# Attention and two expert layers on one core: second halves of x on GpSimd one a unit, a group split later, its four pieces in another order

## The chip, the cores and the metric

The kernel runs on one core of a Trainium2 chip. The metric is device time in microseconds (us), the median over the runs of one kernel. The core has TensorE (PE, with its weight loads as PEld), VectorE (DVE), ScalarE (ACT), GpSimd (POOL) and the queue that issues the DMAs (SP). Each engine works through its own instructions strictly in the order in which the program emits them, so an instruction that waits holds up all that stands behind it on that engine.

## The reference

```python
attn_out = _attn_ref(q, k, v, w1, b1, w2)             # 2 batches, 8 heads, 576 rows, 64 columns
x = attn_out.transpose(0, 2, 1, 3).reshape(1152, 512)
# first layer: w_in 512x2048 and w_out 2048x512
h = x @ w_in
P = a[0] + a[1]*h + a[2]*h**2 + a[3]*h**3
Q = 1.0 + abs(b[0])*abs(h) + abs(b[1])*h**2
x = (P / (Q + 1e-6)) @ w_out
# second layer: 4 experts, w1[e] 512x1024 and w2[e] 1024x512
p = domain_probs / (domain_probs.sum(-1, keepdims=True) + 1e-9)
for e in range(4):
    out += p[:, e:e+1] * (np.maximum(x @ w1[e], 0) @ w2[e])
```

## The kernel before

Every product is made of three: each factor is held as a first part (a copy rounded by ScalarE) and a second part (the factor less its first part, one subtraction on VectorE or GpSimd), and PE adds first*first, first*second and second*first. The change is about who makes second parts, and when.

**The first layer** (loop at L855 and on) has 24 units, each a chunk of 384 tokens (chunks 0 to 2) by 256 of the 2048 inner columns. In unit i PE makes the 24 products `hp` (L56) of x and w_in, and the 24 `yp` of unit i-2. ACT and DVE turn `hp` into g (`chain`, L760 to L777); its last DVE instruction (L777) is the last that reads `hp`, and `hp` has two buffers, so the products of unit i+1 wait for L777 of unit i-1. One weight is split in each unit (`convert`: ACT L369, then the second part in L375). POOL makes the second part of g (L757). The last three f2 of the units go through chunk 2, then 1, then 0. When a chunk's last unit ends (`gather`, L816), DVE adds up its four column blocks d (L826), and `result` (L837) makes the two parts of the new x: ACT L839, then DVE L840. Chunk 2's four results are put into the list `later` and run at the end of that same unit (L874); chunk 1's four and two of chunk 0 are put into `results`, and are taken out one after each of the first three pieces of work of the experts 1 and 2 (L970). The chunk 2 results must be there before the first expert's products.

**The second layer, chunk 2** (loop at L965): for each expert u, `expert_first(u, f2)` makes 24 products `hp` for 256 inner columns, with ACT L847 (`h_hi`) and DVE L848 (`h_lo`) behind them, the last readers of `hp`. Expert u+1's f2 = 0 is made ahead. Then `expert_second(u, t)` makes 24 products `op` for each of three token tiles t, and DVE L896 adds them into `acc`. For the last expert t = 0 and 1 are interleaved: 18 products of each, then 6 of each, then the 24 of t = 2. Two buffers of `hp` again: the products of f2 wait for `h_lo` of f2-2.

**Splitting weights ahead.** Between these, `turns(n)` emits the next n steps of the list `order`; how many stands in `PACE`, three numbers for the places behind `expert_first` 1 to 3 and three for those behind `expert_second` 0 to 2. A weight (`Weight`) is one step: ACT L369, then DVE L375, and then the load of the next but one into the buffer (`stage`, two of them) that this frees. A `Group` holds four blocks of w1[e], for one square below, and is split in five steps (`Group.work`, L400): step 0, ACT L406 and L407 (waits for four DMAs, issued at L398); step 1, three subtractions on DVE or POOL (L410); step 2, four subtractions on POOL, L412 to L415, that turn the four blocks into their sums; step 3, ACT L417 of all four sums; step 4, their second parts, L420: one DVE instruction, or four pieces on POOL in the order 0, 1, 2, 3.

For expert 2 PACE is (2, 1, 1, 3, 3, 3), for expert 3 (2, 2, 2, 2, 1, 2). Around the change this gives, in emission order (W3 are weights of expert 3, G0, G1, G2 the first three groups):

- second layer, expert 2, t = 0; first sums of x (`sums_of_x`: DVE, POOL, DVE, DVE); split of W3 in 3, out 0, out 1
- expert 2, t = 1; split of W3 out 2; G0 steps 0 and 1
- expert 2, t = 2; G0 steps 2, 3 and 4
- expert 3, f2 = 1 (`hp`, `h_hi`, `h_lo`); split of W3 out 3; G1 step 0
- f2 = 2; G1 steps 1 and 2
- f2 = 3; G1 steps 3 and 4
- t = 0 and 1, 18 products each; t = 0, 6 products and its L896; copies of the sums (ACT L954, six); G2 steps 0 and 1
- t = 1, 6 products and its L896; second parts of the sums (DVE L957, six); G2 step 2
- t = 2, 24 products and its L896; G2 steps 3 and 4
- the squares

**The second layer, chunks 0 and 1** (loop at L1064) goes by one level of Strassen's scheme: for each of four experts four squares g, each of seven products m of six matmuls (`Square`, L1001; `sa`, `sb`, `sc`, L1025). They run in the order 1, 6, 7, 2, 5, and 3, 4 of a square after 1, 6 of the next. Product 2 is added onto `sa` and so waits until ACT L1047 has copied product 1; product 5 is added onto `sb` after DVE L1049. Products 6, 7, 5 and 4 use the pieces 3, 1, 0 and 2 of step 4 (`RIGHT`). The fourth group of each expert is split on POOL just ahead of its square.

Of the kernel before, what the change touches and what calls it, by code (L numbers as in the profile page):

```python
# [15 lines left out]
ALU = mybir.AluOpType  # L16
# [31 lines left out]
def attention_then_two_ffn(ctx: ExitStack, tc: tile.TileContext, q, k, v, w1, b1, w2, w_in, w_out, ca, cb, probs, e_w1, e_w2, c_l, c_l8, c_p, c_x, out):  # L48
    nc = tc.nc
    act, dve, pool, pe, sp = nc.scalar, nc.vector, nc.gpsimd, nc.tensor, nc.sync  # L50

    def f32(ap):
        return ap.bitcast(F32)
# [117 lines left out]
    later = []  # L171

    def catch_up(calls):
        now, calls[:] = calls[:], []
        for f in now:
            f()
# [200 lines left out]
    class Group:  # L377
# [22 lines left out]
        def work(self, step, eng):  # L400

            b, s, raw = self.b, self.s, self.raw
            n = 4 if eng is dve else 1
            b11, b12, b21, b22 = (raw[:, i] for i in range(4))
            if step == 0:
                act.activation(b[:, 0, 0], b11, AF.Copy)  # L406
                act.activation(b[:, 2:4, 0], raw[:, 2:4], AF.Copy)  # L407
            if step == 1:
                for i in (0, 2, 3):
                    eng.tensor_tensor(b[:, i, 1], raw[:, i], f32(b[:, i, 0]), ALU.subtract)  # L410
            if step == 2:
                pool.tensor_tensor(b11, b12, b11, ALU.subtract)  # L412
                pool.tensor_tensor(b12, b22, b12, ALU.subtract)  # L413
                pool.tensor_tensor(b22, b22, b11, ALU.subtract)  # L414
                pool.tensor_tensor(b21, b21, b22, ALU.subtract)  # L415
            if step == 3:
                act.activation(s[:, :, 0], raw, AF.Copy)  # L417
            if step == 4:
                for i in range(0, 4, n):
                    eng.tensor_tensor(s[:, i:i + n, 1], raw[:, i:i + n], f32(s[:, i:i + n, 0]), ALU.subtract)  # L420

    W1 = [(Weight(w_in, f2, False), Weight(w_out, f2, True)) for f2 in range(DFF // 256)]
# [30 lines left out]
    def convert(steps=5):  # L453

        for _ in range(steps):
            if state["step"] == 0 and not can_convert():
                return
            i = state["done"]
            if isinstance(order[i], Group):
                if state["step"] == 0:  # L460
                    order[i].place()
                order[i].work(state["step"], side[0])
                state["step"] = (state["step"] + 1) % 5
                if state["step"] == 0:
                    under_way.pop(i)
                    state["done"] += 1
                    load_ahead()
            elif state["step"] < 4:
                under_way[i].narrow(state["step"])
                state["step"] += 1  # L470
            else:
                order[i].place()
                under_way.pop(i).split()
                state["step"] = 0
                state["done"] += 1
                load_ahead()
# [6 lines left out]
    x_t = {}  # L483
# [24 lines left out]
    class Pair:  # L508
# [69 lines left out]
        def parts(self, x):  # L578

            o = self.o  # L580
            yield x[:, 0:512].rearrange("p (k a i) -> p a k i", a=4, i=32), o[:, :, 32:160].rearrange("p a (k i) -> p a k i", i=32)
            for e in range(2):
                r, c = slice(64 * e, 64 * e + 64), 160 * (1 - e)
                yield x[r, 512:S].rearrange("p (a i) -> p a i", i=32), o[r, 2 * e:2 * e + 2, c:c + 32]
# [114 lines left out]
    units = [(n, u) for n in range(NN) for u in range(9)]  # L699
    units[:11] = [(0, u) for u in (0, 1, 2, 3, 4, 5, 8)] + [(1, 0), (1, 1), (0, 6), (0, 7)]  # L700
    for i in range(-2, len(units)):
        if i + 2 < len(units):
            n, u = units[i + 2]
# [5 lines left out]
        if 0 <= i + 1 < len(units):  # L709
            n, u = units[i + 1]  # L710
            pair[n].exp(u)
        if i >= 0:
            n, u = units[i]
# [9 lines left out]
    def first(w, c):  # L723

        wt = ready(w)
        w.left -= 1
        hp = ps.tile([P, 2, 512], F32, tag="s", name="hp")
        for fi in range(2):
            i = 0
            for cc in range(4):  # L730
                for wpart, xpart in ((0, 0), (0, 1), (1, 0)):
                    mm(hp[:, fi, :CHN], wt[:, cc, wpart, 128 * fi:128 * fi + 128], x_t[cc][:, c, xpart], i == 0, i == 11)
                    i += 1
        return hp[:, :, :CHN]
# [4 lines left out]
    units = [(c, f2) for grp in range(NGRP) for c in (range(3), range(2, -1, -1))[grp % 2] for f2 in GROUPS[grp]]  # L739
    CHUNKS = range(3) if NGRP % 2 else range(2, -1, -1)  # L740
# [5 lines left out]
    results = []  # L746
# [13 lines left out]
    def chain(i, h, tile):  # L760

        qd, u, r = tile("qd"), tile("u"), tile("r")
        act.activation(qd, h, AF.Abs, scale=abs_b[:, 1:2])
        act.activation(u, h, AF.Identity, scale=nca[:, 3:4], bias=nca[:, 2:3])
        yield
        dve.scalar_tensor_tensor(out=qd, in0=qd, scalar=abs_b[:, 0:1], in1=h, op0=ALU.add, op1=ALU.mult)
        dve.tensor_tensor(u, h, u, ALU.mult)
        dve.scalar_tensor_tensor(out=u, in0=u, scalar=nca[:, 1:2], in1=h, op0=ALU.add, op1=ALU.mult)
        act.activation(qd, qd, AF.Abs)
        act.activation(r, qd, AF.Ln, bias=one)  # L770

        act.activation(h, r, AF.Exp, scale=-1.0)
        yield

        dve.scalar_tensor_tensor(out=qd, in0=qd, scalar=1.0 + 1e-6, in1=h, op0=ALU.add, op1=ALU.mult)
        dve.scalar_tensor_tensor(out=h, in0=u, scalar=nca[:, 0:1], in1=h, op0=ALU.add, op1=ALU.mult)
        dve.scalar_tensor_tensor(out=u, in0=qd, scalar=-2.0, in1=h, op0=ALU.add, op1=ALU.mult)  # L777
        g_of[i] = u
        yield
# [20 lines left out]
    def tmp(name, dt=F32):  # L800
        return mp.tile([P, 2, CHN], dt, tag="g", name=name, bufs=13)
# [14 lines left out]
    def gather(i):  # L816
        c, f2 = units[i]
        if i not in ends:
            return
        yp = y_of.pop(c)  # L820
        for d in range(4):
            ya = yacc[:, d, CHN * c:CHN * c + CHN]
            if i == first_end[c]:
                act.activation(ya, yp[d][:, :CHN], AF.Copy, scale=1 / WUP)  # L824
            elif i == last_end[c]:
                dve.scalar_tensor_tensor(out=ya, in0=yp[d][:, :CHN], scalar=1 / WUP, in1=ya, op0=ALU.mult, op1=ALU.add)  # L826
                if c != CHUNKS[2] or d > 1:
                    (later if c == CHUNKS[0] else results).append(lambda ya=ya, yt=x_t[d][:, c]: result(ya, yt))
            else:
                if d % 2 == 0:  # L830
                    new = tmp("y")
                act.activation(new[:, d % 2], yp[d][:, :CHN], AF.Copy, scale=1 / WUP)  # L832
                if d % 2:
                    ya = yacc[:, d - 1:d + 1, CHN * c:CHN * c + CHN]
                    pool.tensor_tensor(ya, ya, new, ALU.add)

    def result(ya, yt):  # L837

        act.activation(yt[:, 0], ya, AF.Copy)  # L839
        dve.tensor_tensor(yt[:, 1], ya, f32(yt[:, 0]), ALU.subtract)  # L840

    h_of = {}

    def expert_first(u, f2):
        h = first(W2[u][f2][0], CHUNKS[0])
        hi, lo = tmp("h_hi", F32R), tmp("h_lo", F32R)
        act.activation(hi, h, AF.Relu)  # L847
        dve.scalar_tensor_tensor(out=lo, in0=h, scalar=0.0, in1=f32(hi), op0=ALU.max, op1=ALU.subtract)  # L848
        h_of[u, f2] = hi, lo
# [3 lines left out]
    for i in range(1, len(units) + LAG):  # L853
        on = i < len(units)
        if on:  # L855
            c, f2 = units[i]
            steps = chain(i, first(W1[f2][0], c), tmp)
            next(steps)
        if i <= len(units):
            parts(i - 1)  # L860
        if on:
            convert(STEPS[i][0])
            next(steps)
            convert(STEPS[i][1])
        if not on:

            expert_first(0, i - len(units))
        if i >= LAG:
            second(i - LAG)
            gather(i - LAG)  # L870
        if on:
            next(steps)
            convert(STEPS[i][2])
            catch_up(later)  # L874

    catch_up(later)

    pr_sb = const.tile([P, NT // P, E], F32, name="pr_sb")
    for j in range(NT // P):
# [47 lines left out]
    def turns(n):  # L927

        for _ in range(n):
            if state["done"] < len(order) and state["step"] == 0 and isinstance(order[state["done"]], Weight) and can_convert():  # L930
                state["step"] = 4
            convert(1)
# [28 lines left out]
    for i, a in enumerate((acc_01[:, 0], acc_01[:, 1], acc_2[:, 0])):  # L961
        acc_of[CHN // P * CHUNKS[0] + i] = a

    PACE = {0: (2, 2, 1, 1, 1, 2), 1: (2, 1, 1, 1, 1, 2), 2: (2, 1, 1, 3, 3, 3), 3: (2, 2, 2, 2, 1, 2)}
    for u in range(E):  # L965
        for f2 in range(1, 4):
            if (u, f2) != (0, 1):
                expert_first(u, f2)
            turns(PACE.get(u, PACE[1])[f2 - 1])
            if 0 < u < E - 1 and results:  # L970
# [3 lines left out]
        for t in range(3):  # L974
# [4 lines left out]
            if (u, t) in ((E - 2, 0), (E - 1, 0), (E - 1, 1)):  # L979
                next(making)  # L980
            turns(PACE.get(u, PACE[1])[3 + t])

# [161 lines left out]
```

## Time and profile before

| | |
|---|---|
| median of 3 runs | 796.0 us (793.53 to 797.44) |
| profiled execution, its time | 792.57 us |
| its span in the trace | 790.8 us (1.77 us lie around it) |
| PE busy | 762.3 us |
| DVE, ACT, POOL busy | 558.0, 429.3, 255.2 us |
| granted TensorE clock, mean | 0.998 |

The span is cut by engine; a group of instructions that follow one another on one engine shows as one row with its count. "Idle before" is the time an engine stood still ahead of a row, and the arrow names what ended it.

### The profile page before, as it was taken

To read this page: it belongs to the slowest core of one execution; us is meant where nothing else is said; L and a number is where in the kernel's file an instruction comes from. 1 tells how busy PE (TensorE), PEld (TensorE's weight loads), DVE (VectorE), ACT (ScalarE), POOL (GpSimd) and SP (SyncE) were. 2 spreads that over 40 slices of the span, in tenths; PEclk is the share of its full clock that TensorE was granted. 3 is DMA by queue.
4 is the path that set the end of the run, shared out by engine and by line. 5 is a ranking of instruction groups with operands and counts; after the bars stand their busy time and mean duration, and the time that the engine had idled before them with its cause. 6 is when DMAs were issued, how large, how long until landed. Compare 5 with 4: busy or idle time off the path is not lost. (4 is left out here: it accounts for less than half of the span.)

```text
span 790.8 us, 15912 instructions
## 1 busy us (share of the span) xinstructions
PE 762.3 (96%) x6470; PEld 659.3 (83%) x6470; DVE 558.0 (71%) x883; ACT 429.3 (54%) x689; POOL 255.2 (32%) x268
## 2 busy tenths in 40 slices
PE   8998999989999999999999999899999999999998
PEld 5445666758899999999998989789889989988987
DVE  7988879996999999999854635647545545644631
ACT  6986657765888889786733524234414323413410
POOL 0000223541453656541100000136436534723710
PEclk9999999999999999999999999999999999999999
DMA  8899586551241231401224533332212202212201
GB/s 148 189 219 211 116 199 160 140 110 46 81 133 54 97 117 59 155 13 50 72 81 133 154 110 110 113 100 94 80 54 81 79 29 81 81 42 77 69 27 54
DMA packets 83945, 79.41 MB, mean 100 GB/s; under 512 B 38016, under 2 KB 62976, under 8 KB 83200
## 3 DMA queue, kind: packets, MB, share of 16 engines
q1 hardware_dynamic: 83440, 78.39, 36.5%
q8 instruction: 51, 0.84, 0.4%
q14 instruction: 22, 0.18, 0.1%
q10 hardware_dynamic: 432, 0.01, 0.0%
HBM read 59.20 MB, written 2.36 MB: 78 GB/s over the span
## 5 line engine op out<-in xcount | busy, mean ns | idle before, releaser
L56 PE MATMUL hp<-x,wi 128*128 128x384 f32 x888 | 161.4, 339 | 6.4 <-DVE h_lo L848 3.6
L56 PEld LDWEIGHTS hp<-x,wi 128*128 128x128 f32 x888 | 155.5, 190 | 9.5 <-DVE h_lo L848 3.9
L56 PE MATMUL op<-w,h 128*128 128x512 f32 (+1 forms) x600 | 133.1, 382 | 0.6 <-DVE acc L896 0.6
L56 PEld LDWEIGHTS op<-w,h 128*128 128x128 f32 x600 | 109.5, 188 | 22.4 <-DVE acc L896 0.8
L56 PE MATMUL yp<-g_hi,w 128*128 128x384 f32 x384 | 102.1, 336 | 0.3 <-ACT y L832 0.3
L896 DVE SCALAR_TENSOR_TENSOR acc<-op,pr_sb,acc 128x512 f32<-128x512 f32 (+1 forms) x28 | 20.4, 730 | 73.9 <-PE op L56 73.9
L56 PEld LDWEIGHTS yp<-g_hi,w 128*128 128x128 f32 x384 | 69.7, 188 | 1.3 <-ACT yacc L824 0.6
L536 ACT ACTIVATE pq<-pq,nm 128x576 f32<-128x576 f32 x72 | 55.4, 772 | 22.5 <-DVE nm L527 22.2
L757 POOL TENSOR_TENSOR g_lo<-u,g_hi 128x768 fp32r<-128x768 f32 x24 | 45.2, 1885 | 62.4 <-ACT g_hi L756 55.9
L56 PE MATMUL yp<-g_lo,w 128*128 128x384 f32 x192 | 64.2, 334 | 0.0
L527 DVE CUSTOM_DVE_ANT_0 pq<-sc,ba 128x576 f32<-128x576 f32 x72 | 51.4, 745 | 16.2 <-PE sc L56 16.1
L56 PE MATMUL sc<-ks,qs 64*128 64x288 f32 (+1 forms) x320 | 56.5, 429 | 6.3 <-DVE nm L527 4.7
L373 POOL TENSOR_TENSOR w<-stage,w 128x256 fp32r<-128x256 f32 x64 | 48.1, 782 | 40.0 <-ACT w L369 40.0
L417 ACT ACTIVATE wi<-stage 128x1024 fp32r<-128x1024 f32 x16 | 17.0, 1061 | 80.3 <-POOL stage L415 80.3
L56 PE MATMUL op<-w,h_hi 128*128 128x512 f32 x192 | 59.2, 389 | 0.0
L369 ACT ACTIVATE w<-stage 128x1024 fp32r<-128x1024 f32 x32 | 33.6, 1054 | 36.8 <-DMA stage<-in_moe_w_dram 36.8
L543 DVE STREAM_TRANSPOSE pt<-pq 128x576 f32<-128x576 f32 x72 | 52.3, 753 | 0.0
L576 PE MATMUL o<-pt,val 32*64 32x128 f32 (+1 forms) x2304 | 48.9, 293 | 2.6 <-issue 1.4
L576 PEld LDWEIGHTS o<-pt,val 32*64 32x64 f32 x2304 | 39.3, 130 | 13.1 <-issue 5.2
L1037 ACT ACTIVATE h<-part_sums 128x384 fp32r<-128x384 f32 x48 | 25.1, 522 | 46.2 <-DVE part_sums L1057 36.9
L232 PE MATMUL bps<-hid,wb 128*32 128x288 f32 x576 | 46.9, 410 | 3.3 <-DVE hid L221 2.4
L56 PEld LDWEIGHTS sc<-ks,qs 64*128 64x128 f32 (+1 forms) x320 | 29.8, 175 | 23.2 <-DVE nm L527 10.2
(141 smaller groups left out, 1441.2 us busy)
## 6 DMA issues: line engine op xcount, KB each, us to landing
stage<-in_moe_w_dram SPq DMA_DIRECT2D x48, 512.0 KB, 3.5
ba<-ev SPq DMA_DIRECT2D x32, 288.0 KB, 5.3
words<-in_moe_w_in_dram SPq DMA_DIRECT2D x8, 1024.0 KB, 5.6
words<-in_moe_w_out_dram SPq DMA_DIRECT2D x8, 1024.0 KB, 4.9
stage<-in_moe_w_dram SPq DMA_DIRECT2D x64, 128.0 KB, 2.4
val<-val SPq DMA_DIRECT2D x21, 288.0 KB, 4.0
val<-in_v_dram SPq DMA_DIRECT2D x11, 288.0 KB, 4.7
out_dram<-acc SPq DMA_DIRECT2D x8, 256.0 KB, 2.0
```

The source lines that it names most:

```text
L56: pe.matmul(o, lhsT=l, rhs=r, start=start, stop=stop)
L232: pe.matmul(sc[32 * par:32 * par + 32, hf, :288], lhsT=wb.rearrange("p r h -> p (r h)"), rhs=tiles[par][:, 288 * hf:288 * hf + 288], start ...
L369: act.activation(t[:, :, 0, :], self.raw, AF.Copy)
L373: pool.tensor_tensor(t[:, x[0], 1, x[1]], self.raw[:, x[0], x[1]], f32(t[:, x[0], 0, x[1]]), ALU.subtract)
L417: act.activation(s[:, :, 0], raw, AF.Copy)
L527: dve.tensor_tensor_reduce(out=self.row(u + e).rearrange("p (a j) -> p a j", a=2), in0=o[:, :, :288], in1=bs.rearrange("p (a j) -> p a j", ...
L536: act.activation(self.row(u), self.row(u), AF.Exp, bias=least.pop((self.n, u)), scale=-1.0, accum_out=self.sm[:, u:u + 1])
L543: dve.transpose(self.pt[:, 5 * e + k], self.row(u))
L576: pe.matmul(self.o[64 * e:64 * e + 64, a, c:c + 32 * m], lhsT=val[self.n % 2][r, NKB * e + b], rhs=self.pt[r, i:i + m, 32 * b:32 * b + 32] ...
L757: pool.tensor_tensor(lo, u, f32(hi), ALU.subtract)
L896: dve.scalar_tensor_tensor(out=a, in0=op, scalar=pr_sb[:, j, e:e + 1], in1=a, op0=ALU.mult, op1=ALU.add)
L1037: act.activation(t[:, 0], v, AF.Relu)
```

## The change

Three things: `result` makes the second part on POOL, and all results go through one list, from which one is taken at the end of each unit from the nineteenth on; PACE of the experts 2 and 3; the order of the four pieces of step 4 on POOL.

```diff
             if step == 4:
-                for i in range(0, 4, n):
+                for i in (0,) if n == 4 else (3, 1, 0, 2):
                     eng.tensor_tensor(s[:, i:i + n, 1], raw[:, i:i + n], f32(s[:, i:i + n, 0]), ALU.subtract)
...
                 if c != CHUNKS[2] or d > 1:
-                    (later if c == CHUNKS[0] else results).append(lambda ya=ya, yt=x_t[d][:, c]: result(ya, yt))
+                    results.append(lambda ya=ya, yt=x_t[d][:, c]: result(ya, yt))
...
         act.activation(yt[:, 0], ya, AF.Copy)
-        dve.tensor_tensor(yt[:, 1], ya, f32(yt[:, 0]), ALU.subtract)
+        pool.tensor_tensor(yt[:, 1], ya, f32(yt[:, 0]), ALU.subtract)
...
             convert(STEPS[i][2])
-            catch_up(later)
-
-    catch_up(later)
+            if results and i < len(units):
+                results.pop(0)()
...
-    PACE = {0: (2, 2, 1, 1, 1, 2), 1: (2, 1, 1, 1, 1, 2), 2: (2, 1, 1, 3, 3, 3), 3: (2, 2, 2, 2, 1, 2)}
+    PACE = {0: (2, 2, 1, 1, 1, 2), 1: (2, 1, 1, 1, 1, 2), 2: (2, 1, 1, 2, 2, 3), 3: (2, 2, 2, 2, 3, 2)}
```

## Rows read from the trace of the kernel before

**Rows 1.** Waits of PE: what it waited for, us in total, times, longest.

```profile
PE hp L56 <- DVE h_lo L848: 3.6, 1, 3.6
PE hp L56 <- DVE u L777: 3.3, 5, 1.4
...
PE sb L1025 <- POOL wi L420: 2.1, 4, 0.5
```

**Rows 2.** Timeline of PE, first layer, units of chunk 1: start, us, what.

```profile
354.37 4.33 PE L56 MATMUL hp<-x,wi 128*128 128x384 f32 x24
362.71 4.33 PE L56 MATMUL hp<-x,wi 128*128 128x384 f32 x24
...
381.09 4.33 PE L56 MATMUL hp<-x,wi 128*128 128x384 f32 x24
```

**Rows 3.** Timeline of DVE in the same units.

```profile
362.23 3.62 DVE L840 TENSOR_TENSOR x<-yacc,x 128x384 fp32r<-128x384 f32 x4
...
371.55 0.95 DVE L777 SCALAR_TENSOR_TENSOR u<-qd,hp 128x768 f32<-128x768 f32 x1
```

**Rows 4.** The ten instructions of L840, their durations in ns (min, median, max).

```profile
L840 DVE TENSOR_TENSOR x<-yacc,x x10: 547/551/2214, 362.2 to 484.0; 128x384 fp32r<-128x384 f32 x10
```

**Rows 5.** Timeline of POOL beside them.

```profile
362.55 1.94 POOL L757 TENSOR_TENSOR g_lo<-u,g_hi 128x768 fp32r<-128x768 f32 x1 [7.12 <-ACT g_hi L756]
```

**Rows 6.** POOL's groups by shape: count, busy us, mean ns of one.

```profile
L598 POOL TENSOR_TENSOR x<-x,x 128x384 fp32r<-128x384 f32 x7 | 7.1, 1019 | 0.6
```

**Rows 7.** Timeline of PE, experts 2 and 3 to the first square.

```profile
501.08 8.49 PE L56 MATMUL hp<-x,wi 128*128 128x384 f32 x48
513.17 6.00 PE L56 MATMUL hp<-x,wi 128*128 128x384 f32 x24 [3.60 <-DVE h_lo L848]
519.00 0.63 PE L56 MATMUL op<-w,h_hi 128*128 128x512 f32 x2
...
535.37 1.21 PE L1025 MATMUL sa<-x,wi 128*128 128x384 f32 x6
```

**Rows 8.** Windows: us, busy PE, PEld, DVE, ACT, POOL, granted clock, DMA share, GB/s.

```profile
514.00:519.00 5.00, 5.00 (x21) 5.00 (x21) 1.64 (x4) 1.75 (x3) 0.00 (x0) 0.68 0.64 182
```

**Rows 9.** Timeline of ACT from expert 3 to the first square.

```profile
506.71 0.63 ACT L407 ACTIVATE wi<-stage 128x512 fp32r<-128x512 f32 x1 [1.31 <-DMA stage<-in_moe_w_dram]
...
510.89 0.79 ACT L847 ACTIVATE h_hi<-hp 128x768 fp32r<-128x768 f32 x1
...
534.23 1.06 ACT L417 ACTIVATE wi<-stage 128x1024 fp32r<-128x1024 f32 x1 [6.83 <-POOL stage L415]
...
536.61 0.49 ACT L1047 ACTIVATE part_sums<-sa 128x384 f32<-128x384 f32 x1 [1.32 <-PE sa L1025]
```

**Rows 10.** Timeline of DVE in the same stretch.

```profile
507.37 0.81 DVE L410 TENSOR_TENSOR wi<-stage,wi 128x256 fp32r<-128x256 f32 x2 [1.52 <-ACT wi L407]
...
512.16 0.95 DVE L848 SCALAR_TENSOR_TENSOR h_lo<-hp,h_hi 128x768 fp32r<-128x768 f32 x1
...
518.48 1.66 DVE L410 TENSOR_TENSOR wi<-stage,wi 128x256 fp32r<-128x256 f32 x3
...
528.76 0.75 DVE L896 SCALAR_TENSOR_TENSOR acc<-op,pr_sb,acc 128x512 f32<-128x512 f32 x1 [4.06 <-PE op L56]
529.43 1.63 DVE L410 TENSOR_TENSOR wi<-stage,wi 128x256 fp32r<-128x256 f32 x3
...
531.65 3.83 DVE L957 TENSOR_TENSOR s<-yacc,s 128x768 fp32r<-128x768 f32 x4
...
537.00 1.21 DVE L420 TENSOR_TENSOR wi<-stage,wi 128x1024 fp32r<-128x1024 f32 x1
```

**Rows 11.** Timeline of POOL in the same stretch: the last sum of G1, then of G2.

```profile
521.63 0.73 POOL L415 TENSOR_TENSOR stage<-stage 128x256 f32<-128x256 f32 x1
...
533.26 0.93 POOL L415 TENSOR_TENSOR stage<-stage 128x256 f32<-128x256 f32 x1
```

**Rows 12.** Timeline of PE, product 6 of the fourth square and the product behind it.

```profile
556.17 0.51 PE L1025 MATMUL sb<-s,wi 128*128 128x384 f32 x2
...
558.01 1.21 PE L1025 MATMUL sb<-x,wi 128*128 128x384 f32 x6
```

## The prediction

> **What bounds the kernel now.** PE, busy for 762.3 of the 790.8 us of the span; its three products for one are the work, and the change takes none of them away. So a gain can only come from time in which PE stands still or runs slowly. I read first the waits of PE [rows 1]: the one for `h_lo` (3.6 us, once), the five for L777 (3.3 us, the longest 1.4) and the four for POOL's L420 (2.1 us). Each of the three parts of the change touches one of these. Then I read PE's own timeline at each place, from start to start, because the lost time is more than the wait shows: a restart costs a little, and the clock can fall.
>
> - First layer: a unit takes 362.71 - 354.37 = 8.34 us, yet from 362.71 to 381.09 two units take 18.38, 1.70 too many [rows 2]. DVE explains it: four L840 fill 3.62 us, and L777, for which PE waits, ends only at 372.50 [rows 3].
> - Expert 3: from 501.08 to the first square at 535.37 lie 34.29 us [rows 7]. 48 `hp` last 8.49 and 24 last 4.33 [rows 2, 7], so 24 take 4.16 in a row, and the three sets 12.48. The 72 `op` take 535.37 - 519.00 = 16.37, or 0.227 each. Together 28.85: 5.44 us are lost, 3.60 standing and 6.00 - 4.33 = 1.67 in the 24 products behind the wait [rows 7], over which the granted clock was 0.68, a stretch partly at the lower level of 1.2 GHz and partly at 2.4 [rows 8].
> - Squares: product 6 of the fourth square takes 558.01 - 556.17 = 1.84 us [rows 12] where six matmuls take 1.04 (a quarter of 4.16), so 0.80 is lost, four times 3.2 us.
>
> **Part 1, results on POOL.** It removes ten L840 of 0.55 us from DVE and adds ten instructions of the same shape to POOL, 1.02 us each by L598, which has that shape [rows 6]; ACT's ten copies stay, and no DMA moves. POOL has the room: it stood still for 7.12 us ahead of its L757 [rows 5]. Chunk 2's four now run in four successive units, so in the unit that stalls L777 ends 3.5 us sooner (3.62 less the overlap with its neighbour), at 369.0. PE wants `hp` at 362.71 + 8.34 = 371.05: 2.1 us of room, and the 1.70 is gone. The last chunk 2 result comes in unit 22, more than a unit ahead of the first expert's products: nothing waits for it. What is late next in these units is nothing I can see. Unknown is what POOL's instructions do to DVE's: one of the L840 took 2.21 us instead of 0.55 [rows 4], and it stood beside POOL's L757 at 362.55 to 364.49 [rows 5]. So the bounds are nothing below and 5 x 1.02 = 5.1 us of DVE delay above, 3.0 beyond the room. I take 0, since DVE's only instruction with two inputs in SBUF left in a unit, L375, stands behind L777, while POOL's instruction follows ACT's copy right behind the first part of the same weight, and so should be over by then.
>
> By the Trainium skill (SBUF — State Buffer, section "SBUF: two separate sides") GpSimd and a VectorE instruction with two SBUF inputs lock each other out of a shared port pair for whole instructions. That speaks against this part. The 2.21 us of L840 agrees with it; by it the sum below would lose up to those 3.0 us.
>
> **Part 2, the group later.** With PACE 2 and 2 for 3 and 3, and 3 for 1, the order becomes: t = 0, W3 in 3 and out 0; t = 1, out 1 and out 2; t = 2, G0 steps 0 to 2; f2 = 1; G0 steps 3 and 4; f2 = 2; out 3 and G1 step 0; f2 = 3; G1 steps 1 and 2; t = 0, copies L954, G1 steps 3 and 4; t = 1, L957, G2 steps 0 to 2; t = 2, G2 steps 3 and 4. Work and DMAs are the same; the loads on SP follow the same freed buffers, and only one write of output passes ahead of one of them.
>
> *What goes.* `h_hi` ran at 510.89 because ACT had L417 ahead of it, which waited for POOL's sums [rows 9]; `h_lo` followed at 512.16 [rows 10]. Now ahead of them stand only L407, ending at 507.34, and L410, ending at 508.18. So `h_hi` ends at 507.34 + 0.79 = 508.13 and `h_lo` at 508.18 + 0.95 = 509.13. PE is through with f2 = 2 at 501.08 + 2 x 4.16 = 509.40: in time by 0.27 us, so 5.44 are saved and the squares could begin at 529.93.
>
> *What is late next.* G2. Its L410 stood ahead of the six L957 and now stands behind them. Six products after 36 put L896 of t = 0 at 513.56 + 42 x 0.227 = 523.1. Then DVE does, back to back: L896 0.67 (528.76 to 529.43 [rows 10]), L420 1.13 (1.21 less the same 0.08 of overlap, 0.75 - 0.67), L896 0.67, six L957 at 2 x 0.95 (768 wide, as L848) + 4 x 0.55 (384 wide, as L840) - 6 x 0.08 = 3.6 when POOL is idle, as it now is. So L410 begins at 529.2. From there to POOL's last sum G1 took 522.36 - 518.48 = 3.88 [rows 10, 11]: 533.1. L417 1.06 and L1047 0.49 [rows 9] end at 534.7. Product 2 of the first square is due at 529.93 + 3 x 1.04 = 533.05 and waits 1.6 us. Behind L417, DVE's L420 and L1049 (1.13 + 0.55) end at 535.9, 0.2 after product 5 is due. With about 0.15 for each restart that gives back 2.1. Bounds: nothing, for the chain may be shorter than I can piece together; and, if L957 and POOL slow each other as before (3.83 for the first four [rows 10] instead of 2.7, and 534.19 - 529.43 = 4.76 for the sums [rows 10, 11]), 2.0 more, which makes the wait 3.6 us, as long as the one whose products then lost 1.67: 5.8 in all. I take 2.1, since DVE and POOL are no longer at it at the same time. What follows (the fourth group on POOL) is emitted between the squares and moves up with them. Net 5.44 - 2.1 = 3.3, between -0.4 and 5.4.
>
> **Part 3, piece order.** Nothing is added. Product 6 needs piece 3, which came last of four of some 0.75 us (L415 [rows 11] has the shape); now it comes first, 2.2 us sooner, against 0.52 waited. Product 7 needs piece 1 some 1.04 us after product 6, 0.75 after the first piece, so no wait follows. In full, 3.2.
>
> **The sum.** 1.7 + 3.3 + 3.2 = 8.2 us. Against the profiled execution 792.57 - 8.2 = 784.4; that execution lies 3.4 under the median of the three runs, 796.0, from which I forecast 796.0 - 8.2 = **787.8**.
>
> **Rivals.**
> - *No give-back* (0.13): G2 is in time. 1.7 + 5.4 + 3.2 = 10.3, 785.7. Against it: the 4.4 us of DVE work between `acc` and L410.
> - *All given back* (0.17): the squares wait as long as expert 3 did and the clock falls there. 1.7 + 3.2 = 4.9, 791.1. For it: the slow L957 [rows 10].
> - *It does not do what it says* (0.05): `h_lo` still comes late, since only 0.27 us is spare and L407 ends only after its DMA. With the group ahead of it as before, again 4.9, 791.1; every us of lateness counts once.
> - *POOL holds DVE* (0.12): the moved instructions meet L375 in the five units, 3.0 lost. 8.2 - 3.0 = 5.2, 790.8. One slow L840 in ten is the evidence [rows 4]. The rule of the Trainium skill named above (SBUF — State Buffer) would make this the outcome.
> - *Slower* (0.03): product 2 of the first square waits for L1047 behind L417 behind G2's sums. Each us counts. It makes the kernel slower once all the gains, 10.3, are lost there, that is with 1.67 for the clock and L1047 ending 8.6 us after 533.05, at 541.7. Against it: nothing in the chain is that long.
>
> The forecast itself has 0.50.
>
> **How the numbers follow.** A measurement of this kernel tells some 0.5%, 4.0 us, from no change. The forecast and *no give-back* lie well beyond it; of the three cases at 4.9 to 5.2 some two thirds do: 0.50 + 0.13 + 0.2 = 0.83 less some for the runs' own spread (3.9 us), 0.80. Slower 0.04, same 0.16. The range reaches from *no give-back*, 785.7 less 0.7, to 791.1 with some 1.2 of POOL's 3.0 on top, 792.3.
>
> **What would show it.** Right: PE's wait for `h_lo` is gone and the clock near 507 to 515 stays at 1.0; no wait for L777 over 1 us behind the chunk 2 results; `sb` no longer waits for L420; a new wait of 1 to 2 us of `sa` in the first square, for L1047 (or L957 and L410 ahead of it); ten POOL instructions of about 1.02 us at L840. Wrong: a wait for `h_lo` that stays, the clock under 1.0 at the first square, L375 or L777 drawn out beside POOL's new instructions, or a new wait of PE anywhere else.

## The result and the profile after

The changed kernel takes 785.82 us, median of 4 runs (784.96 to 787.03), against 794.76 of the kernel before (792.67 to 797.44, 4 runs): ratio 0.9887, 95% interval 0.985 to 0.9924. The profiled execution took 785.17 us, its span 783.4 instead of 790.8, 7.4 less. (From L876 on, a line of the changed kernel has a number one lower than before: L1046 is the L1047 of before, L956 is L957.)

Of the waits of PE in the changed kernel, the two that bear on the change (what it waited for, us in total, times, longest):

```profile
PE sa L1024 <- ACT part_sums L1046: 2.0, 1, 2.0
PE hp L56 <- DVE u L777: 2.0, 4, 0.8
```

Against [rows 1] the wait for `h_lo` and the four for L420 are gone, of the five for L777 the longest is gone, and one new wait has come, in the first square. PE's timeline shows what each was worth, from start to start:

```profile
354.53 4.33 PE L56 MATMUL hp<-x,wi 128*128 128x384 f32 x24
...
387.92 4.33 PE L56 MATMUL hp<-x,wi 128*128 128x384 f32 x24
...
499.70 12.75 PE L56 MATMUL hp<-x,wi 128*128 128x384 f32 x72
...
528.65 1.21 PE L1024 MATMUL sa<-x,wi 128*128 128x384 f32 x6
...
530.74 1.20 PE L1024 MATMUL sc<-s,wi 128*128 128x384 f32 x6
533.90 1.32 PE L1024 MATMUL sa<-x,wi 128*128 128x384 f32 x6 [1.96 <-ACT part_sums L1046]
535.25 1.31 PE L1024 MATMUL sb<-s,wi 128*128 128x384 f32 x6
536.40 1.20 PE L1024 MATMUL sa<-x,wi 128*128 128x384 f32 x6
...
552.00 1.20 PE L1024 MATMUL sb<-s,wi 128*128 128x384 f32 x6
553.04 1.20 PE L1024 MATMUL sb<-x,wi 128*128 128x384 f32 x6
```

The kernel before had these starts, PE again:

```profile
389.44 4.33 PE L56 MATMUL hp<-x,wi 128*128 128x384 f32 x24
...
540.57 1.20 PE L1025 MATMUL sa<-x,wi 128*128 128x384 f32 x6
...
542.65 1.20 PE L1025 MATMUL sb<-x,wi 128*128 128x384 f32 x6
```

- First layer, four units: 387.92 - 354.53 = 33.39 us, before 389.44 - 354.37 = 35.07. **1.68 gained** (forecast 1.7).
- Expert 3 to the first square: 528.65 - 499.70 = 28.95, before 34.29 [rows 7]. **5.34 gained** (5.44); the 72 `hp` run through at 12.75 us.
- First square to the first product of the second: 536.40 - 528.65 = 7.75, before 540.57 - 535.37 = 5.20. **2.55 given back** (2.1).
- Product 6 of each fourth square, read at the first of the four: 553.04 - 552.00 = 1.04, before 1.84 [rows 12]. **0.80 gained, four times** (3.2).

Together 1.68 + 5.34 - 2.55 + 3.2 = 7.67; the span fell by 7.4, and 0.16 of the rest is the attention, which ended that much later here (354.53 instead of 354.37). The change does not touch it, and it differs from run to run: in the runs below the same unit begins between 352.47 and 355.22.

### The profile page after: what moved, and what is told of

The parts are those of the page before. It is cut to its first block, busy times and chain, and to the rows that moved or that the text cites. A ratio compares the mean times of both kernels' runs of the same rounds, so it can differ in the third digit from the quotient of the medians.

```text
span 783.4 us, 15914 instructions
## 1 busy us (share of the span) xinstructions
PE 758.9 (97%) x6470; PEld 657.0 (84%) x6470; DVE 550.2 (70%) x873; ACT 429.2 (55%) x689; POOL 268.0 (34%) x278
## 5 line engine op out<-in xcount | busy, mean ns | idle before, releaser
L56 PE MATMUL hp<-x,wi 128*128 128x384 f32 x888 | 159.7, 337 | 1.5 <-DVE u L777 1.1
L757 POOL TENSOR_TENSOR g_lo<-u,g_hi 128x768 fp32r<-128x768 f32 x24 | 45.1, 1881 | 36.9 <-ACT g_hi L756 34.9
```

The source lines that it names most:

```text
L56: pe.matmul(o, lhsT=l, rhs=r, start=start, stop=stop)
L757: pool.tensor_tensor(lo, u, f32(hi), ALU.subtract)
```

## The experiments

**One part at a time.** Three kernels have one part of the diff each, on the kernel before.

Part 1 alone:

```diff
-                    (later if c == CHUNKS[0] else results).append(...)
+                    results.append(...)
...
-        dve.tensor_tensor(yt[:, 1], ya, ...)
+        pool.tensor_tensor(yt[:, 1], ya, ...)
...
-            catch_up(later)
-
-    catch_up(later)
+            if results and i < len(units):
+                results.pop(0)()
```

> The kernel before with part 1 alone: results on POOL, one a unit. My theory: the stretch of two units that took 18.38 us takes 16.7, PE's wait for L777 behind the chunk 2 results is gone, the span falls by 1.7 us to about 789.1; the waits for h_lo (3.6) and for POOL's L420 (4 x 0.5) stay as before. Rival, POOL holds DVE: L375 or L777 are drawn out beside the new POOL instructions and the span falls by under 0.5 us.

Span 790.0, median 791.72 against 793.39 (ratio 0.9981, 0.9955 to 1.0006): the medians alone do not show a gain. The four units take 387.63 - 354.25 = 33.38 us, the full 1.69 less, so the part does what it should. The span fell by 0.8 only, and PE and ACT of this run show where the rest went:

```profile
512.44 6.01 PE L56 MATMUL hp<-x,wi 128*128 128x384 f32 x24 [4.61 <-DVE h_lo L848]
...
506.01 0.63 ACT L407 ACTIVATE wi<-stage 128x512 fp32r<-128x512 f32 x1 [2.44 <-DMA stage<-in_moe_w_dram]
```

G0's four loads were issued 1.7 us earlier than in the kernel before (500.9 to 502.3 instead of 502.6 to 504.1), but the slowest landed 3.7 us after its issue instead of 2.7. L407 waited 2.44 us for it instead of 1.31 [rows 9], and PE's wait for `h_lo` grew from 3.6 to 4.6 us. Two kernels below gain as much in these units and have the old wait (3.8 and 3.5 us), so the late load does not come with the part.

Part 2 alone, the line of PACE:

> The kernel before with part 2 alone: PACE. My theory: the wait for h_lo and the slow clock behind it go (5.4 us), a wait of sa for L1047 of about 2 us comes in the first square and costs some 2.5 with its restart; the span falls by 2.8 us to about 788.0. Rival, the give-back is owed to the other two parts: no wait in the first square, span 785.4.

Span 787.5, median 790.65 (0.9972, 0.9948 to 0.9996). No wait for `h_lo`: 528.21 - 499.35 = 28.86 us to the first square. The wait in the first square is there without the other two parts, and what it costs depends on the clock. PE's rows, then a window of it and the one behind the same wait in the changed kernel (us; busy PE, PEld, DVE, ACT, POOL; granted clock; DMA share, GB/s):

```profile
499.35 12.66 PE L56 MATMUL hp<-x,wi 128*128 128x384 f32 x72
...
528.21 1.21 PE L1025 MATMUL sa<-x,wi 128*128 128x384 f32 x6
...
533.33 1.32 PE L1025 MATMUL sa<-x,wi 128*128 128x384 f32 x6 [1.83 <-ACT part_sums L1047]
...
539.49 1.20 PE L1025 MATMUL sb<-x,wi 128*128 128x384 f32 x6
```

```profile
535.00:540.00 5.00, 5.00 (x21) 5.00 (x20) 2.01 (x4) 1.60 (x4) 2.10 (x4) 0.66 0.61 182
```

```profile
534.00:539.00 5.00, 4.97 (x27) 4.66 (x28) 3.20 (x6) 2.65 (x5) 2.84 (x4) 1.00 0.33 111
```

Behind 1.83 us of standing still the mean granted clock was 0.66 in the first window, as it was 0.68 behind the 3.60 of [rows 8]; in the changed kernel's profile (the second window) it stayed at 1.00 behind 1.96. In part 2 alone the products up to 539.49 took 11.28 us, and before 542.65 - 535.37 = 7.28: 4.0 lost, 1.4 more than the 2.55 above. The rival (the give-back is owed to the other parts) is out.

Part 3 alone, the order of the pieces:

> The kernel before with part 3 alone: the pieces in the order of their use. My theory: product 6 of each fourth square takes 1.04 us instead of 1.84, the four waits for L420 are gone, the span falls by 3.2 us to about 787.6. Rival, the wait only moves to another piece or product: span falls by the 0.5 us or less.

Span 787.2, 3.6 less, 0.3 of it the attention; median 789.44 (0.9942, 0.9915 to 0.9969). Product 6 takes 1.04 us, and no wait for L420 is left:

```profile
555.83 1.20 PE L1025 MATMUL sb<-s,wi 128*128 128x384 f32 x6
556.87 1.20 PE L1025 MATMUL sb<-x,wi 128*128 128x384 f32 x6
```

**Spreading or the other engine?** Part 1 does two things. The next kernel spreads the results and leaves their second parts on VectorE (L840 behind the unit's L375):

```diff
-                    (later if c == CHUNKS[0] else results).append(...)
+                    results.append(...)
...
-            catch_up(later)
-
-    catch_up(later)
+            if results and i < len(units):
+                results.pop(0)()
```

> The kernel before with the results one a unit, but the second parts still on DVE. My theory: what cost was four of them in one unit, ahead of the next chain, not the engine; with 0.55 us a unit L777 ends in time and the span falls by 1.5 to 1.7 us, as with part 1. Rival, the engine matters: DVE's unit of 7.8 us grows to 8.3 to 8.9, PE waits for L777 in these units by up to 0.5 us each, and the span falls by under 0.8 us or not at all.

A miss. It is slower than the kernel before, if by under 1%: span 793.5, median 797.11 against 793.39 (1.0047, 1.0022 to 1.0073); the four units take 392.17 - 352.92 = 39.25 us instead of 35.07. Neither theory had the reason. DVE, POOL and PE of this kernel:

```profile
359.64 1.22 DVE L375 TENSOR_TENSOR wi<-stage,wi 128x1024 fp32r<-128x1024 f32 x1
360.77 2.23 DVE L840 TENSOR_TENSOR x<-yacc,x 128x384 fp32r<-128x384 f32 x1
...
360.74 1.85 POOL L757 TENSOR_TENSOR g_lo<-u,g_hi 128x768 fp32r<-128x768 f32 x1 [6.76 <-ACT g_hi L756]
...
352.92 4.33 PE L56 MATMUL hp<-x,wi 128*128 128x384 f32 x24
...
379.75 4.42 PE L56 MATMUL hp<-x,wi 128*128 128x384 f32 x24 [1.33 <-DVE u L777]
...
...
392.17 4.33 PE L56 MATMUL hp<-x,wi 128*128 128x384 f32 x24
```

L840 begins 0.03 us after POOL's L757 and ends 0.41 us after it: 2.22 to 2.23 us instead of 0.55, in each of the five units that have one. (The other five, in the second layer, have no L757 beside them and take 0.55.) L757 waits for ACT's first part of g, which waits for L777; L375 fills just that time; so L840, put behind L375, meets L757 every time. In the kernel before the same meeting made 1.66 of the 3.62 us of the burst ([rows 3 to 5]).

To test that, the same results on the same engine, but ahead of L375 (edit against the kernel just above):

```diff
+            if results and i < len(units):
+                results.pop(0)()
             convert(STEPS[i][2])
-            if results and i < len(units):
-                results.pop(0)()
```

> The kernel before with the results one a unit, on VectorE, but L840 ahead of the unit's L375 instead of behind it. With L840 behind L375 each took 2.23 us, since GpSimd's L757 had begun 0.03 us sooner. My theory: that meeting, not the 0.55 us of work, is what cost; ahead of L375 it begins before L757 can, takes 0.55, and L777 is in time: the first layer gains 1.4 us as with the results on GpSimd, span about 789.4 where nothing else differs. Rival, VectorE's room in these units is too small for any L840: PE still waits for L777 and L826, span 791 or more.

Median 791.77 against 793.57 (0.9977, 0.996 to 0.9994), span 790.2. The four units take 388.61 - 355.22 = 33.39 us, to 0.01 the time with POOL:

```profile
361.94 0.55 DVE L840 TENSOR_TENSOR x<-yacc,x 128x384 fp32r<-128x384 f32 x1
362.40 1.22 DVE L375 TENSOR_TENSOR wi<-stage,wi 128x1024 fp32r<-128x1024 f32 x1
...
363.04 2.30 POOL L757 TENSOR_TENSOR g_lo<-u,g_hi 128x768 fp32r<-128x768 f32 x1 [6.75 <-ACT g_hi L756]
...
355.22 4.33 PE L56 MATMUL hp<-x,wi 128*128 128x384 f32 x24
...
388.61 4.33 PE L56 MATMUL hp<-x,wi 128*128 128x384 f32 x24
```

L840 takes 0.55, and now L757 is the one held (2.30 instead of 1.85), without a wait of PE behind it. One place in VectorE's queue decides between 1.68 gained and 4.18 lost. The span fell by 0.6 only, since PE came to the first layer 0.85 us later here (355.22 instead of 354.37) and the wait for `h_lo` was 3.8.

The last of this set moves the second parts to POOL and leaves chunk 2's four in one unit:

```diff
-        dve.tensor_tensor(yt[:, 1], ya, ...)
+        pool.tensor_tensor(yt[:, 1], ya, ...)
```

> The kernel before with the second parts on GpSimd, but chunk 2's four still all in one unit. My theory: the four take 1.02 us each one behind the other, meet VectorE's L375 of that unit, which has two inputs in SBUF, and hold it for up to 1 us; L757 begins some 0.7 us later; L777 of the next unit still ends 1 us ahead of the products that wait for it, so the unit of 9.9 us is back at 8.34 and the first layer gains 1.4 us, as with one a unit: the spreading is not what counts, what counts is that VectorE does not stand behind L757. Rival, the four together are the cost on any engine: PE still waits over 0.5 us for L777.

One run of it, 791.37 us, and one of the kernel before, 794.88, so no interval; span 789.6. PE's four units take 388.18 - 354.79 = 33.39 again. DVE and POOL:

```profile
361.51 1.87 DVE L375 TENSOR_TENSOR wi<-stage,wi 128x1024 fp32r<-128x1024 f32 x1
...
359.32 4.93 POOL L840 TENSOR_TENSOR x<-yacc,x 128x384 fp32r<-128x384 f32 x4 [3.49 <-ACT x L839]
```

The four meet L375, which takes 1.87 instead of 1.22, and are drawn out themselves, 4.93 for four of 1.02; there is room for both. So neither the spreading nor the other engine is needed by itself: in the three kernels that gain, no L840 begins on VectorE while GpSimd's L757 runs. (The burst on VectorE ahead of L375, the fourth case, was not tried.)

**The wait in the first square.** If it comes from G2's subtractions standing behind the six second parts of the sums, it goes when they stand ahead:

```diff
-    ... 3: (2, 2, 2, 2, 3, 2)}
+    ... 3: (2, 2, 2, 4, 1, 2)}
```

> The changed kernel with PACE of expert 3 (2, 2, 2, 4, 1, 2): steps 0 and 1 of G2 move ahead of the six second parts of the sums, the group G0 stays where the change put it. My theory: the wait of sa for L1046 in the first square comes from G2's subtractions standing behind those six on VectorE; now L410 starts at about 524 instead of 528.3 and L1046 runs at about 530.3, ahead of the 531.8 at which product 2 is due; the 2.5 us are not lost, span about 781.0. Rival, the wait belongs to the first square itself (GpSimd's sums or the copies are late anyhow): wait stays over 1 us, span 782.5 or more.

Span 781.7, median 783.57 against 793.57: ratio 0.9871, 0.9845 to 0.9897. DVE, ACT and PE:

```profile
524.24 1.64 DVE L410 TENSOR_TENSOR wi<-stage,wi 128x256 fp32r<-128x256 f32 x3
...
526.46 3.84 DVE L956 TENSOR_TENSOR s<-yacc,s 128x768 fp32r<-128x768 f32 x4
...
529.04 1.06 ACT L417 ACTIVATE wi<-stage 128x1024 fp32r<-128x1024 f32 x1 [5.19 <-POOL stage L415]
530.29 0.49 ACT L1046 ACTIVATE part_sums<-sa 128x384 f32<-128x384 f32 x1 [0.19 <-PE sa L1024]
...
529.05 1.21 PE L1024 MATMUL sa<-x,wi 128*128 128x384 f32 x6
...
533.56 1.32 PE L1024 MATMUL sb<-s,wi 128*128 128x384 f32 x6 [0.18 <-DVE part_sums L1048]
534.72 1.21 PE L1024 MATMUL sa<-x,wi 128*128 128x384 f32 x6
```

L1046 now waits for PE, not PE for it. The first square takes 534.72 - 529.05 = 5.67 us, 0.47 over the 5.20 of before instead of 2.55, although VectorE and GpSimd meet again (3.84 us for the first four second parts, as in [rows 10]). What is left is 0.18 us for L1048 and its restart. The rival is out.

The same with one step more ahead:

```diff
-    ... 3: (2, 2, 2, 2, 3, 2)}
+    ... 3: (2, 2, 3, 3, 1, 2)}
```

> The changed kernel with PACE of expert 3 (2, 2, 3, 3, 1, 2): G2's steps 0 and 1 move ahead of the second parts of the sums too, but ScalarE's L417 of G1 now stands ahead of the six copies of the sums and G2's L406 behind them. My theory: G2's L410 starts only at about 526.4, and the second parts of the sums at about 528.7; products 6 and 7 of the first square wait for them by some 0.5 to 1 us and product 2 for L1046 by under 1: span 782 to 783, between the changed kernel and the other order. Rival, only L410 ahead of the six counts: 781.0 as there.

Span 783.1, median 784.51 (0.9892, 0.9863 to 0.992). ACT and PE:

```profile
524.86 0.40 ACT L406 ACTIVATE wi<-stage 128x256 fp32r<-128x256 f32 x1
...
530.47 1.14 PE L1024 MATMUL sb<-s,wi 128*128 128x384 f32 x5 [1.05 <-DVE s L956]
...
535.00 1.31 PE L1024 MATMUL sb<-s,wi 128*128 128x384 f32 x6 [1.02 <-DVE part_sums L1048]
```

L406 stands behind the six copies, as expected, and two waits of 1 us take the place of the one of 2: product 6 for the second parts of the sums (expected), product 5 for L1048 (not expected). Product 2, for which a wait was expected, had none.

The changed kernel itself, once more, on the same chip:

> The changed kernel once more, beside the other two on the same chip: span 783 to 785, ratio 0.989 to the kernel before. In its profile the wait of sa in the first square of about 2 us. My theory of the clock: such a wait may or may not be followed by some us at the lower level; where it is, 1.6 us more are lost.

Median 787.03 against 793.57 (0.9911, 0.9888 to 0.9934), span 784.5. The wait in the first square was 1.8 us, and this time the clock fell behind it:

```profile
534.00:539.00 5.00, 5.00 (x21) 4.79 (x21) 2.58 (x5) 1.34 (x3) 2.80 (x4) 0.66 0.37 117
```

So beside each other on one chip the changed kernel stands at 787.03, and with PACE (2, 2, 2, 4, 1, 2) at 783.57, 3.5 us lower and the fastest version measured. The intervals of the two ratios still overlap (0.9888 to 0.9934 and 0.9845 to 0.9897), with six runs each; the traces show what the difference is made of: 2.1 us in the first square, and the risk of the lower clock behind the wait.

## Why the prediction was right

- **Part 1**, 1.7 forecast, 1.68 measured: L777 ended in time, and POOL took 1.02 us for each in these units, as priced by L598. That POOL would not hold DVE's L375 there was right for the reason given: POOL's L840 ran at 359.07, over by 360.09, ahead of DVE's L375 at 361.25, which kept its 1.22 us. Only five of the ten, those of the first layer, took 1.02 us; the other five, in the second layer, meet an L375 of VectorE and took 1.64 to 1.65, where PE has no wait in either kernel (none from 400 to 500 us). And the prediction took the burst of 3.62 us as one cost. Nearly half of it was the meeting with L757, and the gain did not need POOL.

```profile
359.07 1.02 POOL L840 TENSOR_TENSOR x<-yacc,x 128x384 fp32r<-128x384 f32 x1 [3.47 <-ACT x L839]
...
361.25 1.22 DVE L375 TENSOR_TENSOR wi<-stage,wi 128x1024 fp32r<-128x1024 f32 x1
```

The Trainium skill (SBUF — State Buffer, "SBUF: two separate sides") was cited as speaking against this part. The meetings agree with the exclusive lock it describes, in both directions: 2.23 us for DVE's L840 behind L757, 2.30 for GpSimd's L757 behind L375. What it meant here was the reverse of what the prediction made of it: the results left VectorE, where the lock hit them, for the queue of the very engine that held it.

- **Part 2, what goes**, 5.44 forecast, 5.34 measured. The chain came as worked out, ACT and DVE 1.1 to 1.2 us and PE 1.4 us earlier than in the forecast's frame:

```profile
505.60 0.63 ACT L407 ACTIVATE wi<-stage 128x512 fp32r<-128x512 f32 x1 [1.52 <-DMA stage<-in_moe_w_dram]
506.14 0.80 ACT L847 ACTIVATE h_hi<-hp 128x768 fp32r<-128x768 f32 x1
...
507.00 0.94 DVE L848 SCALAR_TENSOR_TENSOR h_lo<-hp,h_hi 128x768 fp32r<-128x768 f32 x1
```

`h_lo` ends at 507.94 and PE was through with f2 = 2 at 499.70 + 8.32 = 508.02: 0.08 us between them, where 0.27 was forecast. That was hardly enough: the 72 `hp` last 0.09 longer than in part 2 alone (12.75 and 12.66), where 0.19 lay between them, and so go most of the 0.10 missing from the 5.44. The margin was forecast with PE as it stood without part 1, which brings it here earlier; it held because G0's loads were issued 1.2 us earlier too (501.4 to 502.9). A load that lands 1 us later, as in the run of part 1 alone, should bring a wait back; no profile of this order shows one, and it was not tried. The granted clock stayed at 1.00 from 505 to 513.

- **Part 2, what is late next**, 2.1 forecast, 2.55 measured, at the place and in the chain that were named. DVE, POOL and ACT:

```profile
524.65 2.75 DVE L956 TENSOR_TENSOR s<-yacc,s 128x768 fp32r<-128x768 f32 x4
...
528.26 1.09 DVE L410 TENSOR_TENSOR wi<-stage,wi 128x256 fp32r<-128x256 f32 x3
...
531.66 0.72 POOL L415 TENSOR_TENSOR stage<-stage 128x256 f32<-128x256 f32 x1
...
532.42 1.06 ACT L417 ACTIVATE wi<-stage 128x1024 fp32r<-128x1024 f32 x1 [8.77 <-POOL stage L415]
533.38 0.47 ACT L1046 ACTIVATE part_sums<-sa 128x384 f32<-128x384 f32 x1
...
534.65 0.55 DVE L1048 TENSOR_TENSOR part_sums<-sb,part_sums 128x384 f32<-128x384 f32 x1
```

With POOL idle the first four second parts took 2.75 us, not 3.83 [rows 10], as taken. What came out larger is the wait of product 2: due at 530.74 + 1.04 = 531.78, it began at 533.90, 2.12 late, where a wait of 1.6 and a restart of 0.15 were forecast. The sums took 532.38 - 528.26 = 4.12 instead of 3.88, and L410 began 0.39 us ahead of the first square instead of the 0.73 of the forecast (529.93 - 529.2). Product 5 began 535.25 - 533.90 = 1.35 behind product 2 instead of 1.04, with L1048 ending at 535.20, 0.26 after the product was due (forecast 0.2). What the prediction left to a rival, the clock, belongs to the forecast itself as a second outcome: of three profiles with a wait of 1.8 to 2.0 us there, two had the clock at 0.66 behind it.

- **Part 3**, 3.2 forecast and measured, in the changed kernel and alone.

- **The sum**, 8.2 forecast, 7.67 in the four stretches: the time was 785.82 where 787.8 was forecast, inside 785.0 to 792.3. Of the 2.0 between, 1.2 is the start: the forecast goes from 796.0, and beside the changed kernel the one before took 794.76. The medians lie 8.9 apart there and 6.5 apart in the later set (793.57 and 787.03), on either side of 7.67, so the nearness of any one of them to 8.2 is in part luck. And by its time alone the result fits the rival *no give-back* (785.7) better than the forecast; it is the wait in the first square and its 2.55 us that rule this rival out.

## What to carry to other kernels

When an engine finishes early at one place, follow the freed time to the next thing that is due: nearly half of what part 2 won went back 25 us later, because the change had put G2's subtractions behind six others in VectorE's queue. The order that kept both (4 and 1 instead of 2 and 3 as the fourth and fifth numbers of expert 3's PACE) puts them ahead of those six, which were in time even so. And look at which GpSimd instruction begins beside a VectorE instruction with two SBUF inputs: in these runs the one that began second was held until the other was over, so a place one instruction earlier in the queue can be worth more than moving the work to another engine.

## What was not expected of the hardware

The clock does not follow the length of a wait alone. Behind two waits of 1.8 us the mean granted clock of the next stretch was 0.66, behind one of 1.96 at the same place it stayed at 1.00, and behind 3.6 it was 0.68; the products at the lower level (1.2 GHz) cost 1.4 us more in part 2 alone. And the meeting of L840 and L757 repeated itself to a hundredth of a us, 2.22 to 2.23 in all five units with L840 behind L375, and with L840 ahead of it 0.55 in all five: it is set by the order in the queues, not by chance.
